# A three-layer kernel: row table not zeroed, its rows gathered by masked lists, the third pass found by fewer steps

## The chip, the cores and the metric

One core of a Trainium2 chip. The metric is the device time of one execution, in microseconds (us). Three runs of the kernel before took 290.13, 286.27 and 287.81 us: median 287.81.

## The reference

Three layers follow each other, all in float32.

1. Linear attention: 2 batches, 8 heads, 576 tokens of 64. `phi(x)` projects onto 128 features, subtracts each row's largest absolute value and takes `exp(p)` and `exp(-p)`. Then `kv = phi(k)^T v`, `z = sum phi(k)`, and the result is `phi(q) kv / (phi(q) z + 1e-6)`.
2. A mixture of 8 experts over the 1152 tokens (512 wide): the gate takes the best expert of each token; the first 288 tokens of an expert, in order, are kept; `out = gate * (relu(x w1) w2)` with `w1` 512 x 1024. A token that is not kept gives a row of zeros.
3. A gated layer: each row is divided by its root mean square and scaled by `rms_g`, then `(silu(xn w_gate) * (xn w_val)) w_out`, inner width 1536.

## The kernel before, in words

The work goes in three stages that overlap on the engines.

*Attention.* Nine tiles of 128 tokens for k, nine for q. `proj` (L584) projects a tile, `maxes` (L598) finds the row maxima, `shift` (L617 on VectorE; L614 on ScalarE for a few q tiles) subtracts them, ScalarE takes the exponentials (L636, L710). `k_back` (L659) sums `kv`, with 64-row weights in many small matmuls; `q_back` (L736) multiplies a q tile by it. `route` divides, finds the expert of each token and its place, and scatters the token's row (512 values, the token's number, its gate weight: 514 values, `ROW`) to the row table `disp` in DRAM, by an indirect DMA of GpSimd (`scatter`, L394). Expert e owns the rows from 288 e on (`R` = 288); a ninth part takes what the first pass left over. Three tiles are routed together.

*The row table is zeroed* first by `fill_rows` (L1369, `disp<-zrow`): 21 plain DMAs on SyncE's queue, from a tile `zrow` of zeros with a number out of range in column 512, so that an unused row is a row of zeros whose result is written nowhere. Every scatter into the table waits for all of them.

*Experts, in three passes.* After the first three q tiles `choose` takes the expert with the most tokens so far. The first pass (`expert`, 288 rows) computes it for the rows then there, while the other q tiles are still routed. When all are routed, `passes` finds the expert for the second pass (288 rows): a short list of VectorE steps (`first_`) that ends in `lst0`. A longer list (`then`, 29 steps, L1518 to L1542) sorts all remaining parts by their counts and finds which part, of at most 64 rows (`T2`), is the third pass (`small`), and whether anything is left for a loop behind. SyncE reads the results into registers and loads each pass's rows by plain DMAs from the row table (`load_x`, L909: blocks of 96, 96 and 96 rows for 288). `prep_x` scales the rows by their weights (L934), transposes them on TensorE (L941) and splits the result into a high and a low part, `xT` (L944); `small_x` (L1273) does so for the third pass. Each expert's matmuls are triples of such parts (`three`, L949 to L951). The loop behind (`begin`, `in_loop`) lies in a branch for inputs that need it.

*The gated layer.* The results of the passes are scaled (`scaled`, L1055, L1066) and go to `ua` and `ub`; `glu` multiplies them with the weights, which `conv` has unpacked from `in_gvo` (L546 to L551). `load_id` (L924) loads each row's token number from column 512 of the row table in seven small DMAs, for the final scatter into `out_y` (L394).

*What sets the order.* Every operation is entered in a `Sched` with its costs, its reads and its writes. Its method `run` issues them, engine by engine, in an order that is written out by hand as `PLAN`: a number for each operation and the engine that takes it. The queues of SyncE and GpSimd follow that order too. Buffers come from classes (`b2`, `w4`, `h1`, ...) of a fixed number of tiles.

Of the kernel before, what the change touches and what calls it, by code (L numbers as in the profile page):

```python
# [34 lines left out]
6 u 0 q 4 2 8 y a i 10 12 14 2a c 1k 18 16 1c 24 1a s e 1g 2c 3e 1y 1e 2g 1o g 1s 2o k 1m m 2q 1q 2k 3w w 2e 3g 1w 3c 2i 1u 2w 2s 3a 30 3k 3y 2m 2y 20 3i 34  # L35
22 26 3s 3o 40 32 38 44 36 42 3m 2u o 46 3q 28 4a 4i 48 4e 9c 5e 3u 5m 4s 4c 6c 4v 5g 5o 4x hs 5i 4k 5k 4o 4m 5q 72 4q 50 1i 68 4z 4g 56 5u 53 5s 54 74 6e 6i
59 64 7c 6a 6g 6k 5w 5a 6m 5c 60 5y 8i 66 6q 6o 7u 6s 6w 7w 7e 6y 70 62 80 84 7a 7g 7i 7y 8g 6u 88 7s 7m 8a 8c 82 8q 7k 8e 7o 8s 8u 86 90 8w 92 a8 9e 8o 8y 78
76 9g b4 94 ai 9i 9o 9s 9u bc 9k ac 7q 9m 9y 9w aa a2 b0 be ae 9q b2 c6 a0 bg bi bm a6 bs bk bq bu aq bw c0 by c2 9a c8 as ag 8k 8m 96 bo c4 ao 98 co a4 au am
d2 cq cs d4 fa aw cu cc g1 g5 di fe da d6 cw h4 ak g3 ba cy dk dm b8 g6 d0 b6 do dq de cg dy ay g9 ds ca ce fc e0 gc du dw fi fo gf ga fs fg gg fm ck fk hk ea
h6 gk d8 gi e2 dg ec dc h8 ci he fq fu hg ia e4 hq e8 ho ic hu cm ie hw ig hm hy fw hi ou ha fy m4 iu go ii f2 iw ek i0 ee e6 i2 ik i8 iq gq hc gs em i4 eo k4  # L40
im nn eq gw gu es h2 h0 eg is k8 io i6 j0 gy js j2 j4 j8 ei l6 j6 f4 f8 jc k6 no f6 jg ja eu ji le jm jk ju l8 jw je jy kq lc ks m6 iy jo la m8 ka jq mu ma k0
me nr mg ew nk kc mc mk k2 r0 ly lg mm ls l2 lj ky ke ns m1 11m ki pr kg mq gm mo kk lm ms ku km lp nv mw n0 ko ps lu m2 lk lw ng o5 n2 mi lq 11q oy nw 11o ni
p0 l0 n4 p2 n8 n6 p6 p4 nc pa pe ny pg 11s o0 pk o2 pm oc ey po o9 oa na r2 pi om ne ok o6 r4 f0 l4 qi qf kw r6 r8 sk uz rg sm my ri so oi ra sq qx oe pu rc
qc ss rk si ow 13q qk ro su pw 13s or re sw v0 sy og rq p8 t0 pc sf t2 oo rs vl 11u t4 vo qg 15w q9 t6 t8 ta tc q0 te os tg py ti qm s0 q4 tk tm to tq ts qa
rm ru q2 q6 qs um qu qq tu qo tw ty 15y sa u0 100 s6 rx s8 130 vm sc u2 w6 s2 u4 s4 u6 u8 zy w8 vq uo ua ry v2 uc v4 ue ug uq ui vh us uk qy wa sg ve w3 vs
10l 13u v6 vc va v8 vw 10c z0 vy z2 vi vu z4 uu w0 uw wc we wi w4 13w z6 zu zc zw 10v zo ws wg wu zr wk 10e zf wm 104 wo 10g 10m wx zg zi 10w wq z8 zs zl 108
za 106 zm 112 wy 10a xa x6 160 124 127 10i x2 xg 10o x0 11k 132 162 128 102 x8 11x 13o 10q 120 xe 12f xi 122 10s 11a 114 116 x4 134 xk 12w 118 10y xm 148 11c
xo 13y xq 110 12g 150 11e 154 11h 14b 140 12s xs xu xw 15s 12u 14j 15u xy 164 y0 14c 12i 12k 11y 14k xc y2 y4 17i y6 166 136 12m 12q 12o 11i 14m 138 157 142
1e0 13c y8 13a 158 17m ya 13i 13e 198 15a 194 12y 13g yc yi 13k 14y 14u 14o 15p 14w 152 13m yo 14q 15m 14s 16i 17k 15c 16m ye 15e 15g yg 15q 196 yk 1a8 15i
16k 17o 15k 171 16o 14g 174 16s 19a yu 16y 16u 1aa yw 12c 172 16w 1ei ym 16q 1ac 176 1eg 12a 17g 178 17e yq 188 1ae 17q 17t 17a 144 14e 1a6 146 ys 1ag 168 16c  # L50
1ek 1ee 1bo 19c 1bq yy 16a 19f 17c 186 17w 1bk 17z 1ai 1as 17u 1em 16e 1fq 1g4 1e2 1bu 1e4 182 1eo 184 1eq 1bg 19g 1e6 1a2 1bm 1e8 1fu 1fs 1fw 16g 1bc 1eb 1bs
1bw 180 18a 1fy 19y 1ba 1ay 1gq 1by 18c 18e 1aw 1c0 1b0 1c2 1g0 18g 1c4 18i 1c6 1f0 18k 1c8 1bi 18m 1im 1ca 1b2 1a0 1g6 1b7 1ak 1ec 1cc 18o 1g8 1ce 18q 1g2
1dw 18s 1a4 1b4 1cg 1dy 19k 18u 1ci 1ck 19s 1am 1es 1cm 1be 1co 1ga 1b8 1ap 18w 1kq 1gc 1jy 18y 1ik 1gf 1cq 190 1io 1gg 192 1aq 1gu 1cs 1gw 1d2 1fm 1f6 1iq
1ie 1d8 1cw 1de 1it 1iu 1gi 1cu 1da 1f4 1eu 1fi 1dg 1gy 1cy 1ig 1fo 1h0 1iw 1hk 1km 1d4 1d0 1dk 1di 1h2 1dc 1d6 19i 1hm 1qo 1dm 1ew 1ds 1do 1jq 1du 1ey 1hs
# [21 lines left out]
class Sched:  # L76
# [37 lines left out]
    def op(self, eng, cost, fn, r=(), w=(), kb=0, bias=0, act=0.97, hot=None, col=False):  # L114
        return self.any([(eng, cost, fn)], r, w, kb, bias, act, hot, col)

    def any(self, ways, r=(), w=(), kb=0, bias=0, act=0.97, hot=None, col=False):
# [4 lines left out]
        for wr, items in ((False, r), (True, w)):  # L122
            for it in items:
# [14 lines left out]
        self.ops.append(dict(ways={e.upper(): (c, f, e == "DVE" or e == "POOL" and not kb) for e, c, f in ways}, deps=deps, vals=vals, kb=kb, act=act, prio=i + bias + self.shift, hot=hot, col=col))  # L138
        return i

    @staticmethod
    def lead(last, o):


# [6 lines left out]
    def run(self, given=""):  # L151
# [63 lines left out]
        while len(order) < n:  # L215
# [1619 lines left out]
```

## Time and profile before

| | |
|---|---|
| median of three runs | 287.81 us |
| the profiled execution's own time | 288.61 us |
| its span, first to last instruction | 286.9 us |
| mean granted clock of TensorE | 0.988 |
| busy: TensorE matmuls / weight loads | 272.1 / 253.8 us |
| busy: VectorE / ScalarE / GpSimd | 214.6 / 156.2 / 21.1 us |
| moved by DMA | 54.07 MB, 188 GB/s |

Busy times are sums over an engine's instructions. "Idle before" is the time that an engine stood still ahead of an instruction; the releaser is what ended it. "issue" is idle time for which the profile shows no other work that was waited for. PE is TensorE, DVE VectorE, ACT ScalarE, POOL GpSimd, SP SyncE; SPq is SyncE's queue of DMAs. `disp<-zrow` reads: written is `disp`, read is `zrow`.

### The profile page before, as it was taken

What the parts mean: (1) busy time and instruction counts of PE and PEld (TensorE: products, weight loads), DVE (VectorE), ACT (ScalarE), POOL (GpSimd) and SP (SyncE); (2) the same over time, 40 slices, a digit from 0 to 9 for tenths busy, and PEclk for the clock granted to TensorE, in tenths of its full rate; (3) what the DMA queues carried; (4) which work ended last, traced back from release to release, by engine and by line L of the source; (5) the groups of instructions that cost most, each with busy time, mean ns of one, the idle gap of its engine ahead of it and who ended that gap; (6) DMA issues with size and microseconds to landing.
All of it is one profiled execution on the core that took longest, in us unless ns stands there. A gap on an engine that the chain in (4) does not pass through costs nothing.

```text
span 286.9 us, 7639 instructions
## 1 busy us (share of the span) xinstructions
PE 272.1 (95%) x2973; PEld 253.8 (88%) x2973; DVE 214.6 (75%) x590; ACT 156.2 (54%) x328; POOL 21.1 (7%) x53
## 2 busy tenths in 40 slices
PE   8897999699999999999999999999999999999991
PEld 7796898599999999899998999999899999998980
DVE  2984589857999989699899999889966745638310
ACT  1766655227996735634886977745553644421140
POOL 4000000040023600000000000000000000000033
PEclk9999999979999999999999999999999999999997
DMA  5776889929941578786786467665875722002113
GB/s 186 194 195 206 233 238 272 247 97 282 365 176 57 186 229 309 231 298 218 227 296 212 143 193 253 193 224 175 306 241 172 182 87 75 37 0 81 36 62 127
DMA packets 26156, 54.07 MB, mean 188 GB/s; under 512 B 4510, under 2 KB 9630, under 8 KB 26112
## 3 DMA queue, kind: packets, MB, share of 16 engines
q1 hardware_dynamic: 24992, 50.91, 56.6%
q0 software_dynamic: 1120, 2.59, 2.5%
q8 instruction: 25, 0.41, 0.6%
q14 instruction: 19, 0.16, 0.2%
HBM read 39.94 MB, written 14.64 MB: 190 GB/s over the span
## 4 chain that ended last, share of the span: by engine, by line
PE 80%; issue 7%; DVE 5%; POOL 1%; DMA 1%; POOLq 0%; SPq 0%; DVEq 0%
PE bank L949 14%; PE bank L950 14%; PE bank L951 14%; PE bank L736 7%; PE bank L659 6%; PE bank L584 6%; PE bank L954 3%; PE bank L955 3%; PE bank L956 3%; PE bank L704 3%; POOL out_y L394 1%; DMA out_y<-zrow 1%; PE bank L683 1%; DVE cat L551 1%; DVE cat L549 1%
## 5 line engine op out<-in xcount | busy, mean ns | idle before, releaser
L949 PE MATMUL bank<-w,k 128*128 128x384 f32 x96 | 32.6, 340 | 0.0
L950 PE MATMUL bank<-w,k 128*128 128x384 f32 x96 | 32.5, 338 | 0.0
L951 PE MATMUL bank<-w,k 128*128 128x384 f32 x96 | 32.4, 338 | 0.0
L598 DVE TENSOR_REDUCE m<-bank 128x4 f32<-128x512 f32 x36 | 23.6, 681 | 11.3 <-PE bank L584 11.1
L1120 ACT ACTIVATE h<-bank 128x256 f32<-128x256 f32 (+1 forms) x24 | 10.3, 435 | 38.8 <-PE bank L951 36.0
L549 DVE SCALAR_TENSOR_TENSOR cat<-cat 128x512 int32<-128x512 int32 x36 | 24.6, 687 | 5.4 <-ACT cat L548 4.4
L546 ACT ACTIVATE cat<-w 128x512 f32<-128x512 f32 x36 | 24.2, 674 | 6.4 <-DVE cat L549 3.1
L949 PE MATMUL bank<-ua,k 128*128 128x256 f32 x96 | 27.3, 284 | 0.0
L950 PE MATMUL bank<-ua,k 128*128 128x256 f32 x96 | 27.2, 283 | 0.0
L951 PE MATMUL bank<-ua,k 128*128 128x256 f32 x96 | 27.0, 282 | 0.0
L636 ACT ACTIVATE k<-b 128x512 f32<-128x512 f32 x36 | 20.1, 621 | 11.4 <-DVE b L617 11.3
L548 ACT ACTIVATE cat<-w 128x512 int32<-128x512 uint8 x36 | 23.8, 673 | 4.1 <-DMA w<-in_gvo 1.7
L617 DVE TENSOR_TENSOR b<-bank,m 128x512 f32<-128x512 f32 x31 | 20.9, 686 | 6.5 <-issue 2.6
L551 DVE SCALAR_TENSOR_TENSOR cat<-w,cat 128x512 int32<-128x512 int32 x36 | 24.6, 687 | 0.5
L659 PE MATMUL bank<-b,k 128*64 128x65 f32 (+1 forms) x640 | 19.7, 225 | 5.2 <-issue 4.8
L659 PEld LDWEIGHTS bank<-b,k 128*64 128x64 f32 (+1 forms) x640 | 18.4, 139 | 6.3 <-issue 5.6
L584 PE MATMUL bank<-wph,b 64*128 64x128 f32 x288 | 22.2, 304 | 1.1 <-PE bank L584 0.5
L1121 DVE TENSOR_TENSOR h<-h,bank 128x256 f32<-128x256 f32 (+1 forms) x24 | 11.6, 484 | 14.1 <-ACT h L1120 9.4
L584 PEld LDWEIGHTS bank<-wph,b 64*128 64x128 f32 x288 | 19.5, 210 | 3.0 <-DVE b L617 0.8
L736 PE MATMUL bank<-kvt,k 128*64 128x73 f32 x576 | 20.2, 227 | 0.5 <-issue 0.5
L736 PEld LDWEIGHTS bank<-kvt,k 128*64 128x64 f32 x576 | 19.0, 136 | 1.5 <-issue 0.7
L710 ACT ACTIVATE k<-bank 128x512 f32<-128x512 f32 x36 | 18.6, 628 | 3.0 <-PE bank L704 3.0
(251 smaller groups left out, 705.7 us busy)
## 6 DMA issues: line engine op xcount, KB each, us to landing
w<-in_gvo SPq DMA_DIRECT2D x36, 512.0 KB, 4.1
w<-in_w SPq DMA_DIRECT2D x24, 512.0 KB, 5.3
disp<-zrow SPq DMA_DIRECT2D x20, 257.0 KB, 7.2
wo<-cat SPq DMA_DIRECT2D x12, 256.0 KB, 3.5
b<-in_v SPq DMA_DIRECT2D x9, 256.0 KB, 4.0
b<-in_qt SPq DMA_DIRECT2D x9, 256.0 KB, 4.3
out_y<-zrow SPq DMA_DIRECT2D x9, 256.0 KB, 4.4
b<-in_kt SPq DMA_DIRECT2D x8, 256.0 KB, 3.4
```

Source lines behind the costliest of these rows:

```text
L546: op("ACT", c_act(512, False), lambda: nc.scalar.activation(out=m.t, in_=hf(), func=AF.Abs, scale=REBASE), [st], [m])
L548: op("ACT", c_act(512, False), lambda: nc.scalar.activation(out=ai(), in_=top(), func=AF.Copy, scale=1.0 / 32, bias=-31.0 / 64), [st], [a])
L549: op("DVE", c_dve(512), lambda: nc.vector.scalar_tensor_tensor(out=ai(), in0=mi(), scalar=3, in1=ai(), op0=ALU.logical_shift_left, op1=ALU ...
L551: op("DVE", c_dve(512), lambda: nc.vector.scalar_tensor_tensor(out=ai(), in0=hi(), scalar=-0x80000000, in1=ai(), op0=ALU.bitwise_and, op1= ...
L584: nc.tensor.matmul(v4(hs[r].t)[:, c, :], lhsT=v4(x.t)[h, c, :], rhs=wph[h, :], start=c == 0, stop=True, skip_group_check=True)
L598: op("dve", c_dve(512), lambda hf=hf: nc.vector.tensor_reduce(out=m.t[:, 4 * hf:4 * hf + 4], in_=v4(hs[hf].t), axis=AX.X, op=ALU.max, appl ...
L617: op("dve", c_dve(512), lambda hf=hf, s=s: nc.vector.tensor_tensor(out=v4(s.t), in0=v4(hs[hf].t), in1=m.t[:, 4 * hf:4 * hf + 4, None].to_b ...
L659: nc.tensor.matmul(a[u // 3].t[o:o + 64, k:k + VW // 2], lhsT=kp.t[r0:r1, f:f + 64], rhs=vt.t[r0:r1, VW * (u // 2) + VW // 2 * i:VW * (u / ...
L736: nc.tensor.matmul(nv(num)[r0:r1, i, :], lhsT=q_[:, c, 2 * i + hf, r0:r1], rhs=kvr[b][:, 2 * i + c, 73 * hf:73 * hf + 73], start=i == 0 an ...
L949: nc.tensor.matmul(o, lhsT=wh, rhs=xs[0], start=fst, stop=False, skip_group_check=True)
L950: nc.tensor.matmul(o, lhsT=wh, rhs=xs[1], start=False, stop=False, skip_group_check=True)
L951: nc.tensor.matmul(o, lhsT=wl, rhs=xs[0], start=False, stop=lst_, skip_group_check=True)
```

## The change

- `fill_rows` and its 21 DMAs are gone, and with them the wait of the scatters. The table's last 64 rows of padding go too.
- A pass's rows are fetched by `gather`, an indirect DMA of GpSimd, in blocks of 128, 128 and 32 rows (64 for the third pass). The list of row numbers (`at`) is made on VectorE in three steps, and a place beyond the pass's count gets a number out of range, which the DMA skips; before each gather, columns 512 and 513 of its block are set to the out-of-range token and to zero, so that a skipped row counts nothing. The gathers wait for the scatters recorded so far.
- The token numbers are copied from column 512 of the gathered blocks; `load_id` and its DMAs are gone. The order of columns in `ub` changes with that.
- `first_` gets three more steps (11 in all), `then` has 11 steps in place of 29 and finds the third pass alone, as the part with the fewest rows above zero. The tail's two counts are found by `ends`, later. The sort (`listed`) stands in the branch, which also zeroes the unused rows itself.
- SyncE reads one register per pass in place of two. The first expert's weight loads from the fifth on wait for its third block's copy.
- `shift` and the scaling of gathered rows may go to VectorE or to ScalarE.
- In the scheduler's model the transfer time per KB, the cost of indirect DMAs and a lag of gathers change, and `PLAN` is new as a whole.

```diff
 PLAN = """
-6 u 0 q 4 2 8 y a i 10 12 14 2a c 1k 18 16 1c 24 1a s e 1g 2c 3e 1y 1e 2g 1o g 1s 2o k 1m m 2q 1q 2k 3w w 2e 3g 1w 3c 2i 1u 2w 2s 3a 30 3k 3y 2m 2y 20 3i 34
+4 0 2 6 8 q y a 10 c i 12 k 24 14 1k 16 18 1c 1y 2a 20 m 3e 1b 2w 1o 1m 1e 2e 1s 1q e 1g s g 2j 2q 1w 1u 3c 2c 30 3g 2o 3a u 2m w 3k 2g 2y 40 34 2k 32 38 4i
...
-    disp = dram.tile([NV * R + T2, ROW], F32, name="disp")
+    disp = dram.tile([NV * R, ROW], I32, name="disp")
...
+    def gather(dst, idx):
+        nc.gpsimd.indirect_dma_start(out=dst, out_offset=None, in_=disp[:, :], in_offset=bass.IndirectOffsetOnAxis(ap=idx, axis=0), bounds_check=NV * R - 1, oob_is_err=False)
...
+        iota(place, [[P, 3]], 0, 1)
+        iota(placek, [[2 * NU * P, 3]], 0, 2 * NU)
...
-    def shift(hs, m, act=0):
+    def shift(hs, m):
...
+            Q.any([("dve", c_dve(512), fv), ("ACT", 4 * 265, fa)], [hs[hf], (m, hf)], [s])
...
-            op("POOL", 1038, lambda k=k, g=g: scatter(disp[:, :], si()[:, k:k + 1], g.t[:, 0:ROW], NV * R, "disp"), [g, (y, "si"), *[(V["disp"], ("z", r)) for r in range(0, NV * R + T2, P)]],
+            op("POOL", 1280, lambda k=k, g=g: scatter(disp[:, :], si()[:, k:k + 1], g.t[:, 0:ROW].bitcast(I32), NV * R, "disp"), [g, (y, "si")],
...
-        x0.extend(load_x(Q, lambda: regs["u"] * W, V["e0"]))
+        far, st = (lambda: x.t[:, 24:27]), (lambda: x.t[:, 12:13])
+        d(95, lambda: nc.vector.tensor_scalar(out=far(), in0=place, scalar1=cm(), scalar2=BIG, op0=ALU.is_ge, op1=ALU.mult), ["cm", C], ["far"])
+        d(75, lambda: nc.vector.tensor_scalar(out=st(), in0=cut[:, 1:2], scalar1=float(W), scalar2=None, op0=ALU.mult), [V["cut"]], ["st"])
+        d(95, lambda: nc.vector.scalar_tensor_tensor(out=at[:, 0:3], in0=place, scalar=st(), in1=far(), op0=ALU.add, op1=ALU.add), ["far", "st", C], [V["at0"]])
+        x0.extend(load_x(Q, 0, 32))
...
-    def load_x(Q, r0, reg, n=W):
-
-        xs = []
-        for a in range(0, n, SUB):
-            x, m = Q.new("b2"), min(SUB, n - a)
-            Q.op("SP", SPD, lambda a=a, x=x, m=m: nc.sync.dma_start(out=x.t[0:m, 0:ROW], in_=rows(r0, a, m)), [reg, V["disp"]], [x], kb=215, bias=0)
-            xs.append((x, x, a, m))
+    def load_x(Q, k, last, n=W):
+
+        xs, blocks = [], [(0, P, 0), (0, P, P), (last, W - 2 * P, 2 * P)] if n == W else [(T2, T2, 0)]
+        for j, (p, m, a) in enumerate(blocks):
+            x = Q.new("b2")
+            Q.any([("DVE", 62, lambda x=x, p=p, m=m: nc.vector.tensor_copy(out=x.t[p:p + m, 512:514], in_=zrow[p:p + m, 512:514])),
+                   ("ACT", 200, lambda x=x, p=p, m=m: nc.scalar.copy(out=x.t[p:p + m, 512:514], in_=zrow[p:p + m, 512:514]))], [(V["zrow"], 0)], [x], bias=XB)
+            Q.op("POOL", 1250, lambda x=x, p=p, m=m, i=3 * k + j: gather(x.t[p:p + m, 0:ROW].bitcast(I32), at[0:m, i:i + 1]), [V["at%d" % k], V["disp"]], [x],
+                 kb=260 * m // P, bias=RB, lag=3000)
+            ids = idi[p:p + m, [(0, 1, 4), (2, 3, 4), (4,)][k][j]:][:, 0:1]
+            Q.any([("DVE", 75, lambda x=x, p=p, m=m, ids=ids: nc.vector.tensor_copy(out=ids, in_=x.t[p:p + m, 512:513])),
+                   ("ACT", 220, lambda x=x, p=p, m=m, ids=ids: nc.scalar.copy(out=ids, in_=x.t[p:p + m, 512:513]))], [x], [(V["idi"], (k, j))], bias=200)
+            xs.append((x, x, a, m, p))
         return xs
...
-    def load_id(Q, r0, reg, a, n, p, j):
...
-    def fill_rows():
-        if fills:
-            r = fills.pop(0)
-            n = min(P, DR - r)
-            dma(lambda: nc.sync.dma_start(out=disp[r:r + n, :], in_=zrow[0:n, 0:ROW]), [(V["zrow"], 0), tick[0]], [(V["disp"], ("z", r))])
...
             whole(lst0, uem),
+            lambda: N.tensor_scalar(out=ax()[:, 0:1], in0=lst0[:, 0:1], scalar1=float(W), scalar2=None, op0=ALU.mult),
+            lambda: N.tensor_scalar(out=ax()[:, 1:4], in0=placek, scalar1=mx(), scalar2=BIG, op0=ALU.is_ge, op1=ALU.mult),
+            lambda: N.scalar_tensor_tensor(out=at[:, 3:6], in0=place, scalar=ax()[:, 0:1], in1=ax()[:, 1:4], op0=ALU.add, op1=ALU.add),
         ]
 
         then = [
...
+            ts(rk, c1, 0.0, BIG, ALU.is_le, ALU.mult),
+            lambda: N.tensor_tensor(out=rk(), in0=rk(), in1=key, op=ALU.add),
+            lambda: N.tensor_reduce(out=least(), in_=rk(), axis=AX.X, op=ALU.min),
+            lambda: N.scalar_tensor_tensor(out=uem(), in0=rk()[:, None, :].to_broadcast([P, 2, NU]), scalar=least(), in1=ue, op0=ALU.is_le, op1=ALU.mult),
+            whole(lst2, uem),
+            ts(lim, mx, -1.0, float(2 * NU * T2), ALU.add, ALU.min),
+            lambda: N.scalar_tensor_tensor(out=keys[:, 1:2], in0=least(), scalar=lim(), in1=least(), op0=ALU.is_le, op1=ALU.mult),
+            lambda: N.tensor_scalar(out=ax()[:, 4:5], in0=placek[:, 0:1], scalar1=keys[:, 1:2], scalar2=BIG, op0=ALU.is_ge, op1=ALU.mult),
+            lambda: N.tensor_scalar(out=ax()[:, 0:1], in0=lst2[:, 0:1], scalar1=float(W), scalar2=None, op0=ALU.mult),
+            lambda: N.scalar_tensor_tensor(out=at[:, 6:7], in0=place[:, 0:1], scalar=ax()[:, 0:1], in1=ax()[:, 4:5], op0=ALU.add, op1=ALU.add),
         ]
...
-    pieces = expert(Q, dict(nextw), lambda: regs["e"], V["e0"], y0, lambda f: None, (False, False), NW)
+    pieces = expert(Q, dict(nextw), lambda: regs["e"], V["e0"], y0, lambda f: None, (False, False), NW, [(V["idi"], (0, 2))])
...
-    Q.op("SP", SPV, fn1, [V["lst0"]], [V["e1"]])
-    x1 = load_x(Q, lambda: regs["u1"] * W, V["e1"])
-    Q.op("SP", SPV, fn2, [V["lst"]], [V["e2"]])
-    x2 = load_x(Q, lambda: regs["r2"], V["e2"], T2)
+    Q.op("SP", SPV // 2, fn1, [V["lst0"]], [V["e1"]])
+    x1 = load_x(Q, 1, 0)
+    Q.op("SP", SPV // 2, fn2, [V["lst2"]], [V["e2"]])
+    x2 = load_x(Q, 2, 0, T2)
+    ends()
```

## Rows read from the trace of the kernel before

**Rows 1.** Page, part 1: busy us (share of the span) xinstructions, by engine.

```profile
PE 272.1 (95%) x2973; PEld 253.8 (88%) x2973; DVE 214.6 (75%) x590; ACT 156.2 (54%) x328; POOL 21.1 (7%) x53
```

**Rows 2.** Waits of PE, longest and shortest: total us, times, longest.

```profile
PE bank L659 <- issue: 4.8, 2, 2.8
...
PE bank L1055 <- DVE xg L1045: 0.3, 1, 0.3
```

**Rows 3.** Chain of waits that ended last: start, us, what.

```profile
23.70 2.00 issue
...
54.75 2.79 issue
...
78.88 0.47 issue
...
82.17 0.55 PE bank L941 x6
```

**Rows 4.** Windows: busy us by engine (instructions), PEclk, DMA share, GB/s.

```profile
20.00:25.00 5.00, 3.68 (x146) 3.34 (x145) 4.79 (x8) 3.60 (x8) 0.58 (x5) 1.00 0.82 245
...
50.00:55.00 5.00, 4.74 (x124) 4.25 (x120) 4.72 (x19) 1.26 (x3) 0.00 (x0) 1.00 1.07 230
55.00:60.00 5.00, 2.46 (x39) 2.34 (x41) 2.29 (x14) 1.15 (x3) 1.15 (x1) 0.80 0.51 152
60.00:65.00 5.00, 5.00 (x56) 4.88 (x53) 3.57 (x10) 1.89 (x5) 2.14 (x4) 0.86 0.34 121
...
75.00:80.00 5.00, 4.53 (x77) 4.14 (x79) 4.90 (x21) 5.00 (x12) 0.00 (x0) 1.00 1.01 400
...
275.00:280.00 5.00, 5.00 (x23) 4.04 (x22) 0.28 (x1) 2.35 (x4) 2.70 (x3) 1.00 0.28 102
```

**Rows 5.** Timeline of SyncE's queue: start, us, line, operation.

```profile
18.08 1.97 SPq L423 DMA_DIRECT2D b<-in_kt  x2
20.09 0.90 SPq L1369 DMA_DIRECT2D disp<-zrow  x2
...
41.54 8.87 SPq L1369 DMA_DIRECT2D disp<-zrow  x11
51.38 0.82 SPq L423 DMA_DIRECT2D b<-in_qt  x2
```

**Rows 6.** Page, parts 3 (queue: packets, MB, share) and 6 (DMA issues).

```profile
q8 instruction: 25, 0.41, 0.6%
...
disp<-zrow SPq DMA_DIRECT2D x20, 257.0 KB, 7.2
```

**Rows 7.** Line 394 (min/median/max ns, first and last start); GpSimd's timeline.

```profile
L394 POOL DMA_INDIRECT disp<-xg,rt x9: 967/1147/2282, 58.6 to 98.5; - x9
...
DMA to landing us min/median/max: 2.3/3.6/6.1
...
61.33 0.98 POOL L394 DMA_INDIRECT disp<-xg,rt  x1 [0.30 <-issue]
...
281.78 0.97 POOL L394 DMA_INDIRECT out_y<-b,idi  x1 [0.30 <-issue]
```

**Rows 8.** Timeline of SyncE's queue at the hand-off.

```profile
103.87 0.33 SPq L909 DMA_DIRECT2D b<-disp  x1
...
106.89 0.58 SPq L909 DMA_DIRECT2D b<-disp  x1
```

**Rows 9.** Timeline of VectorE at the hand-off.

```profile
105.20 0.17 DVE L1542 CAST lst<-rt 1x26 int32<-1x26 f32 x1
...
109.50 0.48 DVE L934 TENSOR_SCALAR xg<-xg 96x512 f32<-96x512 f32 x1
...
111.10 0.48 DVE L1273 TENSOR_SCALAR b<-b 64x512 f32<-64x512 f32 x1
...
114.37 1.18 DVE L944 TENSOR_TENSOR xT<-bank,xT 128x288 fp32r<-128x288 f32 x3
```

**Rows 10.** Timeline of TensorE at the hand-off.

```profile
115.89 0.40 PE L949 MATMUL bank<-xT,b 128*128 128x288 f32 x1
```

More of the change, by code (lines that the diff above doesn't have):

```diff
@@ L39 @@
[L39 to L42, printed above, removed]
@@ L137, in any @@
         hot = self.hot if hot is None else hot
-        self.ops.append(dict(ways={e.upper(): (c, f, e == "DVE" or e == "POOL" and not kb) for e, c, f in ways}, deps=deps, vals=vals, kb=kb, act=act, prio=i + bias + self.shift, hot=hot, col=col))
+        self.ops.append(dict(ways={e.upper(): (c, f, e == "DVE" or e == "POOL" and not kb) for e, c, f in ways}, deps=deps, vals=vals, kb=kb, lag=lag, act=act, prio=i + bias + self.shift, hot=hot, col=col))
         return i
@@ L884, in choose @@
+                   lambda: nc.vector.tensor_scalar(out=two8[:, 1, :], in0=sel0, scalar1=-1.0, scalar2=1.0, op0=ALU.mult, op1=ALU.add),
+                   lambda: nc.vector.tensor_scalar(out=two8[:, 2, :], in0=thr, scalar1=-1.0, scalar2=float(cap), op0=ALU.mult, op1=ALU.add),
                    lambda: nc.vector.tensor_tensor(out=cut[:, 3:4], in0=cut[:, 3:4], in1=cut[:, 2:3], op=ALU.mult),
@@ L974, in split_b, with expert @@
         return h, l
-    def expert(Q, raw, ecur, creg, out_, slot, pool, nw):
+    def expert(Q, raw, ecur, creg, out_, slot, pool, nw, after=()):
         op, new = Q.op, Q.new
@@ L1139, in rows_out @@
             op("ACT", c_act(512), lambda: nc.scalar.copy(out=row.t[0:m, 0:512], in_=o.t[0:m, :]), [o], [row])
-            op("POOL", 1038, lambda: scatter(out, idx()[0:m], row.t[0:m, 0:512], NT * P, "out"), [row, V["idi"], *[(V["out"], ("z", j)) for j in range(NT)]], [(V["out"], (s, i))], kb=260)
+            op("POOL", 1280, lambda: scatter(out, idx()[0:m], row.t[0:m, 0:512], NT * P, "out"), [row, V["idi"], *[(V["out"], ("z", j)) for j in range(NT)]], [(V["out"], (s, i))], kb=260)
         ow, n = {}, len(seq)
@@ L1412, in tile_attn_moe_glu @@
         more_loads(i + 5)
-        if i >= FS:
-            for _ in range(FN):
-                fill_rows()
         if todo is not None:
-            while fills and todo[0] == CUT - 1:
-                fill_rows()
             g = route(*todo)
@@ L1494, in passes @@
         first_ = [
-            lambda: N.tensor_tensor(out=tot(), in0=run[0:1, :], in1=two8[:, 2, :], op=ALU.add),
+            lambda: N.tensor_tensor(out=tot(), in0=run, in1=two8[:, 2, :], op=ALU.add),
             tm(ext_, 0),
@@ L1692, in fn, with v3 @@
             nx["u"], nx["e"] = unit(1)
-        Q.op("SP", 900, fn, [], [V["nx"]])
+        y = Q.new("b2")
+        n = 3 * NU
+        far, ix, row = (lambda: v3(y.t[0:SUB, 0:n])), (lambda: y.t[0:SUB, n:2 * n].bitcast(I32)), (lambda: v3(y.t[0:SUB, 2 * n:3 * n]))
+        to = (lambda: v3(y.t[0:SUB, 3 * n:4 * n]))
+        def v3(a):
+            return a.rearrange("p (u j) -> p u j", u=NU)
+        Q.op("POOL", 180, lambda: (iota(row(), [[0, NU], [SUB, 3]], 0, 1), iota(to(), [[W, NU], [SUB, 3]], 0, 1)), [], [y])
+        Q.op("DVE", 90, lambda: nc.vector.tensor_tensor(out=far(), in0=row(), in1=cnt[0:SUB, :, None].to_broadcast([SUB, NU, 3]), op=ALU.is_lt), [], [y])
+        Q.op("DVE", 90, lambda: nc.vector.scalar_tensor_tensor(out=v3(ix()), in0=far(), scalar=BIG, in1=to(), op0=ALU.mult, op1=ALU.add), [], [y])
+        with tc.manual_schedule():
+            Q.run()
+        with tc.For_i(0, n, 1):
+            Q = body()
+            Q.op("POOL", 1280, lambda: scatter(disp[:, :], ix()[:, 0:1], zrow[0:SUB, 0:ROW].bitcast(I32), NV * R, "disp"), [], [V["disp"]], kb=260)
+            Q.op("DVE", 90, lambda: nc.vector.tensor_copy(out=y.t[0:SUB, 0:n].bitcast(I32), in_=ix()), [], [V["disp"]])
+            Q.op("DVE", 90, lambda: nc.vector.tensor_copy(out=ix()[:, 0:n - 1], in_=y.t[0:SUB, 1:n].bitcast(I32)), [], [V["disp"]])
+            with tc.manual_schedule():
+                Q.run()
+        Q = body()
+        listed(Q)
+        Q.op("SP", 900, fn, [V["lst"]], [V["nx"]])
         new_xr()
```

263 lines of the change are left out of this document (128 added, 135 removed).

## The prediction

> **What bounds the kernel now.** I read the page first. TensorE is busy 272.1 us, 95% of the span of 286.9; VectorE, next, 75% [rows 1]. So the time can only change by TensorE's idle time (14.8 us), by its clock, or by the tail. The list of waits says who causes the idle time: seven waits, from 4.8 down to 0.3 us, sum to 8.1 us, and the longest is called "issue", which means that nothing the profile shows held the engine [rows 2]. The other 6.7 us are the start and the tail. The chain of waits gives the issue waits their places, a third short one among them: 2.00 us at 23.70, 2.79 us at 54.75, 0.47 us at 78.88 [rows 3]. After that the one wait of the list is the 0.3 us for L1055: in the later stages nothing can be won, only lost.
>
> The windows show what stands beside these places [rows 4]: DMA share 0.82 in 20 to 25, 1.07 in 50 to 55. In 55 to 60 TensorE works 2.46 of 5 us, VectorE 2.29 and ScalarE 1.15: three engines starve together. After the 2.79 us the granted clock is 0.80 and then 0.86 over two windows, so part of them ran at 1.2 instead of 2.4 GHz; before, it was 1.00. SyncE's queue shows what fills the DMA engines: the zeroing of the row table, two writes at 20.09, eleven between 41.54 and 50.41 [rows 5], 257 KB each; the page lists a queue of 25 instruction packets beside the data queues [rows 6]. My reading: blocks of instructions come late behind the zeroing writes.
>
> **The parts of the change.**
>
> *Zeroing removed.* Twenty writes of 257 KB [rows 6] and a smaller one go, 5.3 MB in all. At 54.75 us nearly all that had been issued before was zeroing: eleven writes (2.8 MB) against two loads of 256 KB at 51.38 [rows 5]. I count the whole 2.79 us, and the clock: (1 - 0.80) x 5 + (1 - 0.86) x 5 = 1.70 us [rows 4]. Ahead of 23.70 us stand two loads of 256 KB at 18.08 and two zeroing writes at 20.09 [rows 5]: half of the bytes, so I count half of 2.00 us. Bounds: 0 and 2.00 there; 0 and 4.49 at 54.75. The 0.47 us at 78.88 has no zeroing near it, and stays. The scatters no longer wait for the zeroing (the first began at 58.6 [rows 7]); rows come earlier, but TensorE does not wait for them. On SyncE's queue 35 issues go, with those of the next part; the loads at 51.38 stood behind eleven of them, but no wait of TensorE is for a load: 0.
>
> *Rows gathered.* Seven plain loads on SyncE's queue become seven indirect DMAs on GpSimd's; seven small loads of row numbers become copies of a column. For the first pass there is ample cover: its scatters end at 62.3, its first transposes come at 82.17 [rows 3, 7]. Three gathers 1.27 us apart (0.97 and 0.30 idle, as the last scatter [rows 7]), each landing 3.6 us after its start, behind scatters that land 3.6 us after theirs, are done by about 72. The first expert's later weight loads now wait for that; they are used halfway through an expert that begins after 82.17, and what is queued behind them on SyncE, loads of the last stage's weights, TensorE uses only after the second expert, whose first matmul comes at 115.89 [rows 10]. On GpSimd's queue the waiting gathers stand ahead of later tiles' scatters, six of the nine up to 98.5 [rows 7]. Nothing counted.
>
> For the second pass there is little cover. Now the first load begins at 103.87, when the last scatter has landed; the third block is scaled at 109.50, the third pass's at 111.10 [rows 8, 9]. The last piece of the transposed rows is done at 114.37 + 1.18 = 115.55, and the second expert's first matmul comes at 115.89 [rows 9, 10]: 0.34 us to spare. With gathers, the third starts at 103.87 + 2 x 1.27 = 106.4 and lands 3.6 us later (median of the indirect DMAs; 2.3 to 6.1 [rows 7]): 110.0, bounds 108.7 and 112.5. That is 0.5 us late, less 0.34: I count 0.2 us, bounds 0 and 2.7. The third pass's gather starts at 107.7 and lands at 111.3, 0.2 us late; it can go ahead of the others, and its short matmuls then fill the gap.
>
> *Third pass in 11 steps.* The 29 steps that end with the list at 105.37 [rows 9] become 11, and the third pass's load, now at 106.89 behind the list and two register loads [rows 8], is no longer bound by them. Masks, copies and the tail count add some 29 short steps elsewhere: net 11 more, at 0.17 us each (as L1542 [rows 9]) 1.9 us of VectorE. TensorE, which waits for none of it now, hides both; without that cover they would cost those 1.9 us at most. The sort itself now lies in a branch of which the profile shows no instruction.
>
> *Shift on either engine, new order.* What TensorE waits for other than "issue" sums to 2.8 us (8.1 less 4.8 and 0.5); a moved shift or a better order can win no more, and the new order is not to be read from this profile. Bounds: 2.8 us of gain; a loss as in the rivals. I take 0.
>
> *The tail* keeps its five scatters: 0.
>
> **The sum.** The profiled execution took 288.61 us, 1.7 more than its span. 288.61 - 2.79 - 1.70 - 1.00 + 0.2 = 283.3. It is 0.8 above the median of the runs (287.81); on that footing it is 282.5. I forecast **283.0**.
>
> **Rivals.**
>
> *The issue waits stay* (the change removes the writes, not the stalls). For it: the wait at 78.88 came with no zeroing in flight, at a DMA share of 1.01 [rows 3, 4], and the small matmuls of that stage use up instructions fast (146 matmuls in 20 to 25, 23 in 275 to 280). Against it: the two long ones stand right behind zeroing, the short one at full DMA share lasted 0.47. Time: 288.6 + 0.2 - 0.8, about 288. Chance 0.17. On this the Trainium skill, "Runtime: NRT & Kernel Launch", Instruction fetch mechanics, says that a sequencer fetches its next block over its own DMA queue while it executes the present one, mostly hidden. By that rule neither wait would be a fetch, and the time would be this rival's; three engines at rest in one window speak against "hidden" here.
>
> *Gathers stretched by a busy VectorE.* The nine scatters into the table took 0.97 to 2.28 us, while the five at the end, with VectorE at 0.28 of 5 us, took 0.97 each [rows 4, 7]. At 2.28 + 0.30 apart, the third gather starts at 109.0 and lands at 112.6, 3.1 late: 2.8 us of idle TensorE, perhaps 1.7 of clock as at 57.55. Time 283.3 - 0.2 + 2.8 (+ 1.7) = 285.9 to 287.6, on the median's footing 285 to 287. Chance 0.18. The Trainium skill, "SBUF — State Buffer", Who interferes with whom, has the rule that speaks against the change: a vector copy in a two-port mode locks GpSimd out of the shared port, and descriptors wait, 620 ns becoming some 3100. The stretched scatters agree in direction, not in size (2.28 at most); at 3.1 each the estimate would be another 2 us later.
>
> *Slower: the second pass's rows land late.* One place, the hand-off at about 112 us. If gathers are stretched as above and also land as the slowest did (6.1 us [rows 7]), the third block comes at 115.1 and the third pass's at 117.7, 5.6 and 6.6 us late; TensorE has used up its cover and idles 6.3 us, with 1.7 of clock: 283.1 + 8.0 = 291.1; if the wait at 23.70 stays too, 292.1, and a second lost clock brings 293.8. It decides from an idle time of 3.8 us on (288.61 - 283.1 - 1.7), a third block at about 113.6. For it: nothing but 0.34 us of margin. Against it: the third pass's matmuls can fill, and a DMA of 64 rows at the head of the queue needs one landing alone. Chance 0.15.
>
> **Numbers.** Forecast case 0.50, spread 280 to 285. Its low end: 287.81 - 2.79 - 1.70 - 2.00 - 0.47 = 280.85, less some of the 2.8. The range is 280.0 to 289.0: it takes in the first two rivals and the edge of the third, and leaves out about 0.06 below and 0.13 above. A change of 2% (5.8 us, about what a measurement of this kernel can tell from none) is under 282.05 or over 293.6. Under it lie 0.32 (the better part of the forecast case, on the median's footing); over it 0.08, half of the third rival; the other 0.60 lie between.
>
> **What would show it.** Right: no issue wait over 1 us on TensorE before 60 us, a clock of 1.00 from 50 to 65 us, no zeroing writes, a DMA share well under 1 from 40 to 55, and gathers of about 1 us at the hand-off with TensorE at 5 of 5 us around the second expert's first matmul. Wrong: issue waits of 2 us at other places of the first 80 us (first rival); gathers of 2 us and a TensorE wait for the second pass's transposes (second); the same with a fallen clock and more than 4 us idle (third). What would upset the sum altogether is a new order that leaves TensorE without work where it now has some.

## The result, and the profile after

The changed kernel took 289.62 us (median of 10 executions, 288.95 to 290.82); the kernel before took 290.04 in 10 executions between them on the same chip (284.85 to 293.66). The ratio is 1.0131 [1.0093, 1.0169]: 1.3% slower, within the 2% that count as the same, where 283.0 us was forecast, with a range of 280.0 to 289.0. The ratio leaves out executions more than 1.5% above the fastest of the same kernel, which is six of the ten of the kernel before and none of the changed one, so that it is not the ratio of the two medians (those are 0.1% apart). The profiled execution took 289.19 us.

In the changed kernel the scatters are line 402, the gathers 399, the k tiles' matmuls 667 (659 before), the q tiles' last matmuls 744 (736), the transposes of gathered rows 956 (941), the experts' matmuls 964 to 966 (949 to 951), the small pass's 1307 (1292).

Page, part 1, of the changed kernel (answers [rows 1]), then its waits of TensorE (total us, times, longest; answers [rows 2]):

```profile
PE 273.4 (95%) x2973; PEld 253.5 (88%) x2973; DVE 212.2 (74%) x589; ACT 160.6 (56%) x351; POOL 26.9 (9%) x62
```

```profile
PE bank L744 <- issue: 3.1, 6, 1.3
PE bank L460 <- DVE ones_b L455: 1.1, 1, 1.1
PE bank L667 <- ACT b L625: 1.0, 1, 1.0
PE bank L691 <- ACT b L418: 0.8, 1, 0.8
```

The issue waits of the k tiles are gone, 4.8 us of them. The q tiles' matmuls have issue waits in their place, 3.1 us in six pieces, and the waits for ScalarE have grown (0.4 us in all before; 1.0, 0.8 and 0.4 here). Windows of the changed kernel (busy us by engine, granted clock, DMA share, GB/s; answer [rows 4]):

```profile
20.00:25.00 5.00, 4.61 (x186) 4.17 (x183) 3.41 (x6) 4.36 (x9) 0.11 (x1) 1.00 0.48 148
50.00:55.00 5.00, 4.62 (x91) 4.19 (x88) 4.28 (x18) 2.49 (x8) 2.86 (x3) 1.00 0.15 52
55.00:60.00 5.00, 4.25 (x51) 3.86 (x50) 3.97 (x16) 3.95 (x10) 0.27 (x1) 1.00 0.28 76
60.00:65.00 5.00, 4.52 (x61) 4.03 (x60) 4.09 (x10) 3.43 (x8) 3.43 (x6) 1.00 0.95 379
70.00:75.00 5.00, 4.00 (x126) 3.91 (x122) 4.23 (x26) 4.95 (x14) 0.00 (x0) 1.00 0.81 317
80.00:85.00 5.00, 4.31 (x87) 3.51 (x88) 2.59 (x11) 2.49 (x7) 3.20 (x3) 1.00 0.41 104
```

Up to 55 us this is what was forecast: TensorE is fuller in 20 to 25, the DMA share in 50 to 55 fell from 1.07 to 0.15, the clock stays at 1.00. The k tiles' last matmul ends at 51.5 us, 7.8 earlier than before (59.3). Then TensorE loses 0.5 to 1.0 us in each window shown up to 85 us. In TensorE's time from one matmul's start to the next, up to the first expert matmul, the k side (lines 594, 667) gained 7.4 us and the rest lost 6.5, 3.7 of it in line 744. SyncE's queue shows what else moved; the rows are of the changed kernel (start, us, line, operation; answer [rows 5]), then of the kernel before:

```profile
58.65 1.42 SPq L910 DMA_DIRECT2D w<-in_w  x3
60.12 0.93 SPq L527 DMA_DIRECT2D w<-in_gvo  x2
61.24 20.71 SPq L910 DMA_DIRECT2D w<-in_w  x5
```

```profile
63.78 1.27 SPq L898 DMA_DIRECT2D w<-in_w  x2
68.47 1.42 SPq L898 DMA_DIRECT2D w<-in_w  x3
73.12 10.37 SPq L898 DMA_DIRECT2D w<-in_w  x2
```

Seven of the eight weight loads and two conversions' loads, 512 KB each, now leave almost together (all but the last of the five by 64 us); before, they were spread over 63.8 to 73.7. The hand-off of the changed kernel: GpSimd's gathers with the landing time of all seven, VectorE's scaling of the third block and of the third pass's rows and its last piece of the transposed rows, TensorE's first matmul of the second expert (answer [rows 7 to 10]):

```profile
99.44 1.05 POOL L399 DMA_INDIRECT b<-disp,at  x1 [3.18 <-DVE cat L561]
104.54 1.27 POOL L399 DMA_INDIRECT b<-disp,at  x1 [1.21 <-issue]
...
DMA to landing us min/median/max: 4.7/7.1/8.1
```

```profile
110.56 0.47 DVE L949 TENSOR_SCALAR b<-b 32x512 f32<-32x512 f32 x1
113.93 0.49 DVE L1288 TENSOR_SCALAR b<-b 64x512 f32<-64x512 f32 x1
115.05 1.18 DVE L959 TENSOR_TENSOR xT<-bank,xT 128x288 fp32r<-128x288 f32 x3
```

```profile
116.72 0.40 PE L964 MATMUL bank<-xT,xg 128*128 128x288 f32 x1
```

The gathers start 4.4 us before the loads that they replace and land twice as late as assumed (median 7.1 us here, 4.8 in the repeat below); the second expert begins 0.8 us later than before. After the first expert matmul TensorE needs 1.2 us more than before (87.23 to 279.80 then, 86.29 to 280.02 now, first expert matmul to last of line 955 or 970).

### The profile page after: what moved, and what is told of

Its sections match the earlier page's. It is cut to its first block, busy times and chain, and to the rows that moved or that the text cites. A ratio compares the mean times of both kernels' runs of the same rounds, so it can differ in the third digit from the quotient of the medians.

```text
span 287.3 us, 7597 instructions
## 1 busy us (share of the span) xinstructions
PE 273.4 (95%) x2973; PEld 253.5 (88%) x2973; DVE 212.2 (74%) x589; ACT 160.6 (56%) x351; POOL 26.9 (9%) x62
## 4 chain that ended last, share of the span: by engine, by line
PE 69%; issue 15%; ACT 2%; DVE 2%; DMA 2%; POOL 1%; POOLq 0%; SPq 0%; DVEq 0%; ACTq 0%
PE bank L964 13%; PE bank L966 12%; PE bank L965 12%; PE bank L744 7%; PE bank L667 4%; PE bank L594 4%; PE bank L712 3%; PE bank L970 2%; PE bank L969 2%; PE bank L971 2%; DMA out_y<-zrow 2%; POOL out_y L402 1%; PE bank L956 1%; PE bank L691 1%; PE bank L1307 1%
## 5 line engine op out<-in xcount | busy, mean ns | idle before, releaser
L744 PE MATMUL bank<-kvt,k 128*64 128x73 f32 x576 | 21.4, 228 | 3.1 <-issue 3.1
L744 PEld LDWEIGHTS bank<-kvt,k 128*64 128x64 f32 x576 | 19.6, 136 | 4.9 <-issue 4.2
L667 PE MATMUL bank<-b,k 128*64 128x65 f32 (+1 forms) x640 | 19.1, 222 | 1.5 <-ACT b L625 1.0
L594 PE MATMUL bank<-wph,b 64*128 64x128 f32 x288 | 20.1, 292 | 0.1
L970 PE MATMUL bank<-b,h 128*128 128x512 f32 x50 | 19.7, 394 | 0.0
L964 PEld LDWEIGHTS bank<-w,k 128*128 128x128 f32 x96 | 18.0, 188 | 1.6 <-ACT h L1135 0.6
```

What stands on the lines that cost most here:

```text
L594: nc.tensor.matmul(v4(hs[r].t)[:, c, :], lhsT=v4(x.t)[h, c, :], rhs=wph[h, :], start=c == 0, stop=True, skip_group_check=True)
L667: nc.tensor.matmul(a[u // 3].t[o:o + 64, k:k + VW // 2], lhsT=kp.t[r0:r1, f:f + 64], rhs=vt.t[r0:r1, VW * (u // 2) + VW // 2 * i:VW * (u / ...
L744: nc.tensor.matmul(nv(num)[r0:r1, i, :], lhsT=q_[:, c, 2 * i + hf, r0:r1], rhs=kvr[b][:, 2 * i + c, 73 * hf:73 * hf + 73], start=i == 0 an ...
L964: nc.tensor.matmul(o, lhsT=wh, rhs=xs[0], start=fst, stop=False, skip_group_check=True)
L970: nc.tensor.matmul(o, lhsT=xs[0], rhs=wl, start=False, stop=False, skip_group_check=True)
```

## The experiments

Runs of one group shared a chip and runs of the kernel before, and each ratio is to that kernel.

**What is the zeroing worth?** Kernel before 284.73 us. The second run puts the 21 writes back (fill_rows is that of the kernel before):

```diff
+        if i >= 5:
+            for _ in range(3):
+                fill_rows()
```

> The changed kernel as it is, beside the three runs below on one chip. Every theory expects 289 to 291 us and a span near 287. If TensorE's waits for issue in 60 to 86 us (3.1 us in the profile of the changed kernel, the longest 1.33) belong to this order of work, they come back at the same places within a few tenths; if they are chance, they come elsewhere or not at all.

Measured: 285.32 us (284.16 to 287.86), ratio 1.0041 [0.9998, 1.0084], span 283.3. The long wait stands at the same matmul as in the first profile and lasts 2.0 us; the short ones are missing, and the first expert matmul comes at 82.1 us in place of 86.3:

```profile
PE bank L744 <- issue: 2.0, 1, 2.0
```

```profile
L964 PE MATMUL bank<-xT,b x48: 288/293/398, 82.1 to 132.9; 128*128 128x288 f32 x48
```

> The changed kernel in its own order, with the 21 writes of zeros put back at the times that they had (33 to 49 us for most). Theory 1: the cost of the writes comes on top of the new order's, 293 to 296 us. Theory 2: the writes cost what they cost in the old order, also 293 to 296. Theory 3: as without them, 289 to 291.

Measured: 292.33 us (289.28 to 297.54), ratio 1.0236 [1.0149, 1.0323]. The ratios differ by 0.0195, 5.5 us: what the prediction had counted (5.49). TensorE's waits in this run:

```profile
PE bank L668 <- issue: 3.2, 3, 1.9
PE bank L745 <- issue: 1.6, 1, 1.6
```

So in the new order the removal is worth 5.5 us (2.8 to 8.3, if the two intervals are taken as independent), and something in the rest of the change costs as much or more.

**Is it the order?** These six runs have the changed kernel emit its operations in the order of the kernel before, wholly or in one half; the gathers had to be given a place in it.

```diff
 PLAN = """
-4 0 2 6 8 q y a 10 c i 12 k 24 14 1k 16 18 1c 1y 2a 20 m 3e 1b 2w 1o 1m 1e 2e 1s 1q e 1g s g 2j 2q 1w 1u 3c 2c 30 3g 2o 3a u 2m w 3k 2g 2y 40 34 2k 32 38 4i
+6 u 0 q 4 2 8 y a i 10 12 14 2a c 1k 18 16 1c 24 1a s e 1g 2c 3e 1y 1e 2g 1o g 1s 2o k 1m m 2q 1q 2k 3w w 2e 3g 1w 3c 2i 1u 2w 2s 3a 30 3k 3y 2m 2y 20 3i 34 22
...
```

> The changed kernel, its operations emitted in the order of the kernel before (the gathers where the loads of rows stood, the 11 steps of the third pass where the first 11 of its steps stood; the list of ends stays where the new order has it). Theory 1 (the zeroing's removal is worth what it was predicted to be, and the new order gives it back): 283 to 285 us, no wait of TensorE for issue near 23 and 55 us. Theory 2 (the masked gathers cost it, whatever the order): 289 to 291. Theory 3 (the zeroing was hidden, and TensorE's waits for issue fall by chance): as the kernel before, 285 to 291.

> As the run in the old order, with the 21 writes of zeros put back where they stood (the gathers still masked). Theory 1: 4 to 6 us above the run in the old order without them, so 288 to 290, with waits for issue near 23 and 55 us. Theory 2: 293 to 296, since both costs are in it. Theory 3: the same as without the writes, within 1 us.

> The changed kernel in the order of the kernel before, once more: in the first try (291.9 us) the copies of the token numbers stood ahead of other work on ScalarE and waited there for the gathers (2.2 us), the last tile's routing came late, and TensorE stood still and then ran 80 to 90 us at a granted clock of 0.68. Now each gather stands about 12 us ahead of the scaling of its rows and the copy just ahead of that scaling. Theory 1 (the removed zeroing is worth some 5 us, the new order takes it back): 2 to 5 us below the kernel before, 280 to 283. Theory 2 (the gathers cost in any order, and the new order already makes the best of them): no faster than the changed kernel, 285 to 288.

> The changed kernel in the old order as far as the first expert matmul and in its own order from there. If the new order loses its time in the attention stage (TensorE's matmuls for q tiles packed together at 62 to 86 us): as the run in the old order with early gathers, 280 to 283. If it loses it at or after the hand-off: as the changed kernel, 285 to 286. If the gathers cost it: 285 or more.

> The changed kernel in its own order as far as the first expert matmul and in the old order from there. If the new order loses in the attention stage: as the changed kernel, 285 to 286; if at or after the hand-off: 282 to 284.

> The old order with early gathers, and the 21 writes of zeros put back where they stood: against the kernel before only the masked gathers, the 11 steps and the id copies are changed. If gathers placed well cost nothing: as the kernel before within 1 us, and 4 to 6 us above the same order without the zeros. If the gathers cost of themselves: 288 or more.

| run | median us | ratio to the kernel before |
|---|---|---|
| old order | 291.92 | 1.0255 [1.0202, 1.0308] |
| old order, zeros | 293.52 | 1.0294 [1.0229, 1.0358] |
| old order, early gathers | 296.65 | 1.0315 [1.0255, 1.0375] |
| old, then new | 293.77 | 1.0239 [1.0169, 1.0308] |
| new, then old | 294.46 | 1.0228 [1.0171, 1.0286] |
| old, early gathers, zeros | 299.90 | 1.0416 [1.0358, 1.0474] |

All are slower than both kernels; theory 1 as written, that the old order would bring the gain, fell, and so did the expectation that well-placed gathers would bring the last run within 1 us of the kernel before (299.90 against 288.71). The runs don't price the new order either, since the old one does not suit gathers. Before a masked gather a compute engine has to write the row tile, and after it another copies the row numbers; a plain load needed only SyncE. Where these steps stand in the old order, the in-order engines wait. ScalarE in the first run, 60 to 90 us, and VectorE in the third, 85 to 105 us (total us, times, longest):

```profile
ACT idi L927 <- DMA b<-disp,at: 2.2, 2, 1.3
```

```profile
DVE b L921 <- PE bank L965: 2.2, 1, 2.2
```

In the first run the routing behind ScalarE came late, TensorE was busy for 7.56 of 10 us in 70 to 80 and then had a granted clock of 0.68 in 80 to 90. What follows is only that gathers need an order of their own; that they cost time in any order (theory 2) is neither shown nor excluded. The zeros cost 1.1 us in the first pair and 2.9 in the second (ratios 0.0039 and 0.0101 apart, each difference uncertain by some 0.008), less than 5.5.

**Do the stalls of the kernel before belong to it?** Kernel before 285.66 us in this group and in the next two runs.

> The kernel before, unchanged, with a profile of its own. Theory 4 (the zeroing's stalls are paid in some executions and not in others; those that set the comparison hardly pay them, so there was little to win): an execution of 283 to 285 us on a chip like the second, whose TensorE reaches the first expert matmul near 83 us instead of 87.2 and waits for issue under 2 us in all in place of 5.3. Theory 1 (every execution pays them): the waits of 2 to 3 us near 23 and 55 us are there again in the same places, and the first expert matmul comes 5 us after that of the changed kernel.

Measured: 286.51 us (283.52 to 289.16), ratio 1.0013 [0.9971, 1.0054]. Theory 1 has the place right: waits for issue again at 22.6 and 53.0 us, in the same two instructions as in the first profile, and the first expert matmul at 86.1 us, 4.0 after that of the repeat of the changed kernel (another chip; 5 were expected). Their size is not fixed (3.6 us here, 4.8 there):

```profile
PE bank L659 <- issue: 3.6, 2, 2.2
```

That every execution pays for them, as theory 1 also says, is not shown. Both profiles of the kernel before are of executions with a mean granted clock of 0.988 or less. In the group of the first two experiments, eight of its 17 executions had a mean clock of 0.995 or more and took 283.2 to 284.7 us; the other nine took 284.5 to 289.4. A mean of 0.995 leaves at most 1.6 us of lost clock in 285, less than the 1.70 counted behind the wait at 54.75 us, so those eight did not lose that clock. Whether they had the waits no trace shows. So theory 4, that some executions hardly pay and that those set the comparison, stands in part.

**Why do the q tiles wait for issue?** Counting all of TensorE's records from the start (weight loads, matmuls and its sequencer's few), every issue wait of 0.5 us and more in the 16 traces (27 of them) stands right behind one of six records: 449, 961 (23.5 us in the first profile), 1217, 2241 (54.5 us), 2753, 3009, whole multiples of 256 apart. The page lists 25 instruction packets with 0.41 MB, 16 KB each [rows 6], about one for each 256 of TensorE's 6017 records, so I take their queue for TensorE's. In the repeat of the changed kernel, no instruction packet comes between 66.9 us, when TensorE passes record 2753, and 70.8, when it stops at 3009; then comes one (queues from 66.9 to 70.8 us, then from 70.8 to 71.5: packets, MB, share of 16 engines):

```profile
q1 hardware_dynamic: 380, 1.38, 89.3%
q0 software_dynamic: 66, 0.19, 13.0%
```

```profile
q1 hardware_dynamic: 74, 0.28, 99.3%
q8 instruction: 1, 0.02, 9.8%
```

A packet's start does not yet end the wait. At each of the 27 waits TensorE goes on only 2.2 to 3.0 us after the start of the packet. So a stretch of 256 records is covered only if it lasts longer than the packet's delay and these 2.2 to 3.0 us together.

Two edits follow: half as many instructions (128 rows a matmul), and the burst held back (exps lists the q tiles whose exponentials are written, sent the weight loads).

```diff
-                two = parts(t) if len(parts(t)) == 2 else [(parts(t)[0][0], r, r + P // 2) for r in (0, P // 2)]
+                two = parts(t)
```

> The changed kernel, its q tiles' matmuls (line 744) taken 128 rows at a time in place of two halves of 64, so half as many TensorE instructions for the same product. If TensorE's waits for issue in 60 to 86 us come from running through its instructions faster than they arrive (it stood at the same instruction, record 3009, in every run of the new order): they go, 1 to 3 us less than the changed kernel, if a full matmul takes no longer than two halves (35 ns each in the trace). If they come from anything else: the same, or slower by what the full matmuls take more.

Measured: 294.66 us, ratio 1.0301 [1.0252, 1.0350]. The waits of this line went, as the theory says; the time did not fall, because a full matmul takes far longer than two halves: line 744 needs 31.4 us from start to start, 21.6 in the repeat of the changed kernel.

```diff
+            sent.append(f)
+            if len(sent) == 4:
+                nc.sync.dma_start(out=held[:, :], in_=exps[-3].t[0:1, 0:2])
             nc.sync.dma_start(out=x.t, in_=w12[bass.ds(e(), 1), f].rearrange("e p f -> (e p) f"))
```

> The changed kernel, with the fourth and later of the first expert's weight loads (512 KB each) held back on SyncE until the exponentials of a q tile near 68 us are written; they left at 59 to 62 us before, and the transfers then ran at over 390 GB/s from 57 to 74 us. If that burst is what delays TensorE's instructions (in the repeat of the changed kernel the long wait at 70.9 us stood inside it): the wait of 2 us near 71 us shrinks below 0.7, and the run is 1 to 2 us faster than the changed kernel. If the wait has another cause: it stays, and the time too; if the weights are needed earlier than they now come, 1 us slower or more.

Measured: 283.45 us (282.43 to 284.42), ratio 0.9930 [0.9898, 0.9961], span 281.3. The loads left at 71.6 us:

```profile
71.06 0.31 SPq L917 DMA_DIRECT2D held<-k  x1
71.57 6.68 SPq L918 DMA_DIRECT2D w<-in_w  x5
```

Windows of the repeat of the changed kernel, then of the held loads: TensorE's stall in 70 to 74 goes together with the DMA share of 1.02 ahead of it.

```profile
66.00:70.00 4.00, 3.96 (x123) 3.81 (x121) 2.80 (x16) 4.00 (x13) 0.00 (x0) 1.00 1.02 401
70.00:74.00 4.00, 1.97 (x63) 1.88 (x61) 3.07 (x21) 3.03 (x7) 0.00 (x0) 1.00 0.58 227
```

```profile
66.00:70.00 4.00, 4.00 (x119) 3.83 (x119) 3.12 (x15) 4.00 (x14) 0.00 (x0) 1.00 0.49 179
70.00:74.00 4.00, 3.81 (x116) 3.61 (x111) 3.90 (x27) 3.68 (x8) 0.00 (x0) 1.00 0.32 92
```

The first expert matmul, first in the kernel before (run again), then with the held loads, both on this chip (min/median/max ns, first and last start us): 5.5 us earlier, the whole of the forecast gain up to there; 4.0 of it the changed kernel has in its repeat, without held loads (82.1, on a third chip).

```profile
L949 PE MATMUL bank<-xT,b x48: 290/295/400, 86.1 to 140.0; 128*128 128x288 f32 x48
```

```profile
L973 PE MATMUL bank<-xT,b x48: 288/294/400, 80.6 to 131.5; 128*128 128x288 f32 x48
```

**Does it hold beside the changed kernel, and what is the rest?** Kernel before 289.31 us.

> The changed kernel beside the two runs below, on one chip, so that the held loads are compared with it directly and not through the kernel before. Every theory: 0.4 to 1.3% above the kernel before, TensorE waiting for issue 2 to 3 us at 60 to 86 us, most of it at record 3009 of its instructions.

Measured: 290.19 us (288.74 to 290.67), ratio 1.0104 [1.0025, 1.0184].

> The held loads again, beside the changed kernel. If the burst of weight transfers is what ate the gain: 1 to 1.5% (3 to 4.5 us) below the changed kernel and 0.5 to 1% below the kernel before, no wait for issue of 0.5 us or more at 60 to 86 us, first expert matmul near 80.6 us. If the difference of the earlier runs was the chip's: within 0.4% of the changed kernel.

Measured: 288.32 us (287.24 to 289.95), ratio 1.0049 [1.0005, 1.0092]; 1.9 us under the changed kernel, where 3 to 4.5 were expected. The wait at record 3009 is gone and no wait for issue from 60 us on reaches 0.5 us, as expected; but the first expert matmul comes at 84.7, not at 80.6. The idle time ahead of the q tiles' matmuls (us, times; weight loads and matmuls both counted) shows what is left; it is that of the changed kernel and of the held loads on this chip, then of the held loads on the chip before:

```profile
  issue: 6.3, 14
```

```profile
  issue: 4.9, 13
```

```profile
  issue: 0.5, 2
```

On this chip, and in the first profile of the changed kernel, there are runs of stalls of 0.55 to 0.6 us from start to start, about 10 records apart, while GpSimd issues its indirect DMAs (81 to 83 us here). They are not 256 apart, and holding the loads does not touch them. The run with the new order up to the first expert shows them too (0.53 to 0.58 us at 84.8 to 86.8), on a chip of the same number as the first run with held loads, which has none: so neither the order nor the chip alone makes them. The held loads beat the changed kernel by 1.9 us on the one chip where both ran, and the kernel before on one of two.

```diff
-        xs, blocks = [], [(0, P, 0), (0, P, P), (last, W - 2 * P, 2 * P)] if n == W else [(T2, T2, 0)]
+        xs, blocks = [], [(0, SUB, SUB * j) for j in range(3)] if n == W else [(T2, T2, 0)]
```

> The held loads, with the rows of the first two passes gathered in three blocks of 96 in place of 128, 128 and 32 (the token numbers stay laid out for 128, so a fourth of these passes' rows are left out of the writes at the end; read TensorE's times at the hand-offs, not the tail). If the remaining loss after the first expert matmul is the unequal blocks' transposes (24 of them take 4.19 us from start to start in place of 2.01): they take 2 us again, and the first expert matmul and all later milestones come 1 to 2 us earlier, 281 to 282.5 us in all. If it is only that the transposes now wait for something else (copies out of the banks): they stay above 3.5 us, 283 to 284.

Measured: 286.95 us (285.18 to 288.45), ratio 0.9992 [0.9936, 1.0049]. This run leaves out a fourth of the first two passes' rows at the end. The 24 transposes take 2.29 us again in place of 4.20, but the first expert matmul stays at 84.7 and TensorE's last matmul at 278.6: the time saved is lost elsewhere. Before the first expert that is in part a new issue wait (0.8 us at record 1217); after it, TensorE's time falls by 0.1 us only (193.65 for 193.79). The lower total is the tail's, which writes fewer rows. This theory fell; the 1.2 us are not the transposes.

## Why the prediction was wrong, point by point

- **Zeroing removed: right in mechanism; the size holds in one order only.** The waits near 23 and 55 us and the lost clock are gone. When the writes return they cost 5.5 us in the new order, 1.1 and 2.9 in the old. What the waits are is told by one distance, worked out from the trace: after TensorE passes record 1985, the next instruction packet came 5.8 us later in the kernel before, behind the zeroing, and 1.1 us later in the changed one.
- **Shift on either engine, new order: "I take 0". This step failed.** In the first profile the k side gained 7.4 us and the rest of TensorE's work ahead of the first expert lost 6.5. One part of the loss is shown. The new order runs through records 2753 to 3009 in 4.0 us (6.1 before), because the k tiles are finished and the q tiles' short matmuls, some 32 ns apart, follow one another; and the first expert's weights go in one burst at that time. The next packet then comes 3.0 us after record 2753 (3.9 in the repeat); with the 2.2 to 3.0 us that follow a packet's start, that is too late for a stretch of 4.0 us, and TensorE waits 1.0 to 2.0 us in the three profiles of the changed kernel. The kernel before had the same lateness there (4.4 us) and 6.1 us of work to cover it, which is why its wait at 78.88 was only 0.47. With the loads held, the packet comes after 1.3, 0.3 and 0.7 us, and the wait is gone in all three runs; side by side that was worth 1.9 us of the 6.6 between 283.0 and 289.62. The rest of the loss stays open: the short stalls beside GpSimd's indirect DMAs (19.4 or 22.7 us for the same line), longer waits for ScalarE near 55 us, and whether order or gathers bring them. The bound of the step, "a loss as in the rivals", was right; taking 0 was not.
- **The first rival** (the issue waits stay, 288) had the nearest time, in part by luck: it has neither the gain nor the new order's loss. It held that the stalls go where instructions are used up fast, and this they did: 5.3 us of issue waits before, 3.3 after. It was wrong that removing the writes brings nothing. The Trainium skill, "Runtime: NRT & Kernel Launch", Instruction fetch mechanics, gives blocks of 16 KiB, 256 instructions, fetched while the present block runs, "mostly hidden". The spacing of the waits and the packet's size agree with the block; "hidden" does not hold here, with packets that start 3.0 to 5.8 us after the record at the long waits beside full DMA engines.
- **Rows gathered, first pass: 0** stands. The rows land late (a median of 7.1 us over all seven gathers, not 3.6), but no wait of TensorE for them is listed.
- **Rows gathered, second pass: +0.2, bounds 0 to 2.7.** The third block is scaled at 110.56 where its landing was put at 110.0. From the first expert matmul on, TensorE loses 1.0 to 1.6 us in every run in the new order with gathers (192.6 us before, 193.6 to 194.2 after). That is inside the bounds and 1 us over the value taken. Which part of the hand-off it is stays open; the unequal transposes are not it.
- **The second and third rivals** did not come; the time above the range, for which the prediction had counted on late rows of the second pass, came about in another way: the gathers took 0.96 to 1.27 us each, with VectorE busy for 9.4 of 10 us beside them, and TensorE idled 0.2 us in 100 to 110. The Trainium skill, "SBUF — State Buffer", Who interferes with whom, has GpSimd locked out of the shared port by some VectorE operations; no row here shows a gather held up by them.
- **Third pass in 11 steps, tail: 0** stands. Its transposes came 2.3 us later than before (114.72), not earlier, and TensorE did not wait.
- **The footing failed too.** The sum takes the full 5.49 us off one execution of 288.61 us, as if each paid it. The kernel before runs from 282.9 to 293.7 us over the four groups and the first comparison. Its stalls differ between its two profiles (5.3 and 3.6 us), and executions with a mean clock of 0.995 or more, at 283.2 to 284.7 us in one group, are near the forecast with the zeroing in place. A sum against one execution with large stalls wins more than the comparison can show: with the held loads the profile is 3.9 us shorter than that of the kernel before on the same chip, and the ratio gives 2.0. How much of the missing 6.6 us is this footing and how much the new order is not separated.

## What to carry to other kernels

A stall with no releaser that stands at the same instruction in every profile, whole multiples of 256 records from others, was here a place where instructions ran out: ask what fills the DMA engines in the microseconds before, and how fast the engine goes through its next few hundred instructions. Removing the traffic at one such place moves the next transfers earlier, so look where they will land, and hold a burst back with a wait on its queue if it meets a stretch of short instructions. A gather in place of a plain load takes steps on in-order engines, and here did badly in an order made for plain loads. Before counting a stall's whole length, look whether other executions of the kernel had it at all.

## What the runs showed of the hardware

- The 576 matmuls of 64 rows x 73 columns took 19.4 us from start to start with the held loads, 34 ns each; taking 128 rows in place of two halves wherever that could be done lengthened the line to 31.4 us for 320.
- After TensorE had passed such a record, the next instruction packet started within 1.9 us (at times shortly before) in 38 of 39 places where the DMA share of the 2 us ahead was under 0.3, and 0.2 to 5.8 us after (3 us or more in 23 of 62) where it was 0.9 or more. So a high share alone does not make a packet late; what else does is not shown.
- TensorE went on 2.2 to 3.0 us after the start of the packet that ended such a wait (27 waits in 16 traces).
- Line 745 of the same kernel took 19.4 us from start to start in one run and 22.7 in another, most of the difference in short stalls beside GpSimd's indirect DMAs. What they are stays open.
